# Attention with a 64-wide causal window and a ReGLU feed-forward: the first tile's matmuls in another order

## The chip, the cores and the metric

The kernel runs on one core of a Trainium2 chip. Its time is the device time of one execution in microseconds (us); three runs of the kernel before gave 301.91 (median), between 301.77 and 302.06. One further execution was recorded by the hardware profiler: all rows of the profile and of the trace are from it, and their times count from the start of its span.

The names in the profile: PE is TensorE's matmuls and PEld its weight loads, DVE is VectorE, ACT is ScalarE, POOL is GpSimd, SP is SyncE. L589 is line 589 of the kernel.

## What is computed

Two steps, one behind the other. First attention for 8 batches, 8 heads, 576 positions and 64 elements per head, in which a position sees itself and the 63 before it:

```python
scores = scale * np.matmul(q, k.transpose(0, 1, 3, 2))
mask = (rel >= 0) & (rel < 64)                  # rel = query position - key position
attn = softmax(np.where(mask, scores, -1e9))
attn_out = np.matmul(attn, v)
x = attn_out.transpose(0, 2, 1, 3).reshape(4608, 512)
```

then a gated feed-forward on its 4608 tokens of 512:

```python
gate = np.maximum(x @ w_gate, 0.0)              # w_gate 512 x 1536
val = x @ w_val                                 # w_val  512 x 1536
out = (gate * val) @ w_out                      # w_out 1536 x 512
```

Inputs and output are float32; the kernel's matmuls take fp16 and add up in fp32.

## The kernel before, in words

**Tiles and units.** The tokens are cut into small tiles of 384 at the start (`TT`) and large ones of 512 behind them (`WT`). A small tile has two units of 192 tokens (`U`); a unit is what attention works on: scores (`u_st`), exponentials on ScalarE (`u_exp`), masks on VectorE (`u_mask`), the product with v (`u_pv`), then the normalization by the sums (`u_recip`, `u_norm`) and a transposition (`u_turn`) that writes `xt`, the transposed input of the feed-forward. A unit's normalization and transposition come in two halves of four heads: the first half fills the chunks 0 and 1 of `xt`, the second half the chunks 2 and 3 (a matmul's contraction of 512 is done in 4 chunks of 128). For the second half of unit 1 the normalization is done on ScalarE by six operations (`u_norm_act`, L369), all else on VectorE.

**Feed-forward of the small tiles.** `hidden` (L557) computes outputs in blocks of 128 of the 1536, four at a time: first four of w_gate, each four matmuls (one per chunk, L589) into one of four PSUM banks that are taken in turn, with a ReLU by ScalarE to `pr` (L572) behind each; then the same four of w_val, with the product `pr` x bank by VectorE to `g_sb` behind each (the gate, L575). An output of w_gate in the next group writes a bank that a gate must have read before. For the first tile, `hidden(0, ((0, U), (U, TT)), 0, 4, 4)` does the first four outputs for unit 0 and then for unit 1, in matmuls of 192 tokens, two outputs to a bank; the other two groups of four take both units in matmuls of 384. Then come the first unit of the next tile, and `output`, the product with w_out (L1023). The large tiles use `fast_hidden`, `fast_output` and, for the last ones, the class around L847, which do the products by fewer, added-up submatrices named P1 to P7.

**Loads of weights.** `w_load` (L154) brings a group of four outputs in two transfers on GpSimd's queue: chunks 0 and 1, then chunks 2 and 3. All of these queue behind each other and behind loads of q, k and v on the same queue.

**Who sets the order.** Each engine runs its instructions in the order in which the program issues them. The class `Weaver` decides it when the program is built: it holds a clock and a heap of pieces of work with due times (`W.at`); `W.advance(t)` issues what is due until t and moves the clock on. `hidden` advances the clock by the length of its matmuls; `w_need` advances it to the time at which a weight group is planned to have landed (`w_done`). So a piece of attention, a transposition or a gate may be issued in another place when the clock changes upstream, although its own line does not. For the last large tiles the order of the pieces is written out by hand in `SEVEN` (L1069): P5a and P5b are two parts of P5, of four matmuls each, v0, v1, s0, s1 and h1 are pieces of attention and of the previous tile.

**What goes before.** The start (L1083 to L1135) computes the scores of units 0 and 1, with a few matmuls of no result (`heat`, `keep_hot`) between, normalizes and turns unit 0, then unit 1, issues the loads of the second and third groups of weights, and plans the scores of unit 2 at 23.2 on the planner's clock.

Of the kernel before, what the change touches and what calls it, by code (L numbers as in the profile page):

```python
# [10 lines left out]
FP32 = mybir.dt.float32  # L11
FP16 = mybir.dt.float16
ACT = mybir.ActivationFunctionType
MUL = mybir.AluOpType.mult
# [33 lines left out]
def kernel(  # L48
# [10 lines left out]
    nc = tc.nc  # L59
# [4 lines left out]
    U = 192  # L64
    UB = S // U
    NU = B * UB
    NC = DM // 128
    NF = DF // 128
    G = 4
    scale = 1.0 / float(D) ** 0.5  # L70
    TT = 2 * U
    WT = 512
# [12 lines left out]
    g_sb_p = ctx.enter_context(tc.tile_pool(name="g_sb", bufs=2))  # L85
    f_sb = ctx.enter_context(tc.tile_pool(name="f_sb", bufs=3))
# [6 lines left out]
    wg = persist.tile([128, NC, DF], FP16)  # L93
    wv = persist.tile([128, NC, DF], FP16)
# [46 lines left out]
    W = Weaver()  # L141
# [4 lines left out]
    def xt_tile(t):  # L146
        if t not in xts:
            xts[t] = x_sb.tile([128, NC, WT], FP16, name="xt")
        return xts[t]


    w_done = {}

    def w_load(wt, src, f0, f1, landed):  # L154

        if wt is not wo:
            ns = slice(128 * f0, 128 * f1)
            for a in range(2):
                nc.gpsimd.dma_start(wt[:, 2 * a:2 * a + 2, ns], src.rearrange("(a p e) n -> a p e n", a=2, e=2)[a, :, :, ns])  # L159
        if wt is wo:  # L160
            nc.gpsimd.dma_start(wo[:, f0:f1], src.rearrange("(c p) n -> p c n", p=128)[:, f0:f1])
        w_done.update(((wt.name, f), landed) for f in range(f0, f1))

    def w_need(wt, f):
        while (wt.name, f) not in w_done:
            W.pop()
        W.advance(w_done[wt.name, f])

# [52 lines left out]
    def heat(n, to, start=True):  # L223

        for _ in range(n):
            nc.tensor.matmul(to, zero[:, 0:128], zero[:, 0:to.shape[1]], start=start, stop=start, skip_group_check=not start)
# [9 lines left out]
    def one_bank():  # L236
        taken["one"] += 1
        to = singles[(taken["one"] - 1) % 4]
        while id(to) in unread:
            W.pop()  # L240
        return to
# [100 lines left out]
    def pv_of(d, u, hh):  # L342
        return d["pv"][hh][:, 0:SB * VW].rearrange("p (s c) -> p s c", c=VW)

    def u_recip(u, hhs=(0, 1)):
        d = units[u]
        if "r" not in d:
            d["r"] = a_n.tile([128, 2, SB, 1], FP32, name="r")
        for hh in hhs:
            nc.vector.reciprocal(d["r"][:, hh], pv_of(d, u, hh)[:, :, D:D + 1])  # L350

    def u_norm(u, hh):

        d = units[u]
        if "x" not in d:
            d["x"] = xus[:, u % 2].rearrange("p h (s e c) -> p h s e c", e=2, c=D // 2)
        nc.vector.tensor_tensor(d["x"][:, hh], pv_of(d, u, hh)[:, :, 0:D].rearrange("p s (c e) -> p s e c", e=2),
                                d["r"][:, hh, :, :, None].to_broadcast([128, SB, 2, D // 2]), MUL)
        if u >= 6:
            read(d["pv"][hh], True)  # L360

    def u_norm_act(u, hh):

        d = units[u]
        if "x" not in d:
            d["x"] = xus[:, u % 2].rearrange("p h (s e c) -> p h s e c", e=2, c=D // 2)
        pv = pv_of(d, u, hh)
        for s in range(SB):
            nc.scalar.activation(d["x"][:, hh, s], pv[:, s, 0:D].rearrange("p (c e) -> p e c", e=2), ACT.Copy,  # L369
                                 scale=d["r"][:, hh, s])  # L370

    def u_turn(u, hhs=(0, 1)):

        d = units[u]
        c0 = U * (u % 2)
        h0, h1 = hhs[0], hhs[-1] + 1
        for hh in range(h0, h1):
            dst = xt_tile(u // 2)[:, 2 * hh:2 * hh + 2, c0:c0 + U].rearrange("p e (s c) -> p s e c", c=32)
            nc.vector.transpose(dst, d["x"][:, hh])
        if h1 == 2:  # L380
            del units[u]
            if u < 4:
                normed[0] = (u + 1) // 2 - 1
            elif u % 2:
                for n in range(4):
                    W.at(W.clock + 0.5 + 0.9 * n, lambda n=n: x_form(u // 2, n))
# [20 lines left out]
    def part_written(banks):  # L407
        written.update((id(to), 0) for to in banks)

    def read(to, give):  # L410
        unread.discard(id(to))
        if give:
            free.append(to)
# [86 lines left out]
    def x_form(t, n):  # L500

        HT = widths[t] // 2
        xt, xc = xt_tile(t), xc_tile(t)[:, :, :, 0:HT]
        b11, b12, b21, b22 = (xt[:, 2 * k:2 * k + 2, HT * h:HT * h + HT] for k in range(2) for h in range(2))
        x, y = ((b12, b11), (b22, xc[:, 0]), (b22, b12), (b21, xc[:, 1]))[n]
        (nc.vector if t <= NS or t - 1 in FAST_OUT else nc.gpsimd).tensor_tensor(xc[:, n], x, y, SUB)
        if n == 3:
            normed[0] = t
# [42 lines left out]
    gs = {}  # L551
# [2 lines left out]
        while normed[0] < n:  # L554
            W.pop()

    def hidden(t, spans, f0=0, f1=NF, each=1):  # L557

        if t not in gs:
            gs[t] = g_sb_p.tile([128, NF, WT], FP16, name="g_sb"), {}  # L560
        g_sb, done = gs[t]
        xt = xt_tile(t)
        n = spans[0][1] - spans[0][0]

        w = 512 // n
        each = max(each, w)

        def part(tile):
            return tile[:, 0:w * n].rearrange("p (w n) -> p w n", w=w)

        def relu(r_sb, h1):
            nc.scalar.activation(part(r_sb), part(h1), ACT.Relu)  # L572

        def gate(f, c0, r_sb, h2):
            nc.vector.tensor_tensor(g_sb[:, f:f + w, c0:c0 + n], part(r_sb), part(h2), MUL)  # L575
            done.update(dict.fromkeys(range(f, f + w), c0 + n))

        for fb in range(f0, f1, each):
            r2s = [f_sb.tile([128, 2, WT], FP32, name="pr", bufs=4) for _ in range(2)]
            r_sbs = {}  # L580
            for i, wt in enumerate((wg, wv)):
                for c0, f in ((c0, f) for c0, _ in spans for f in range(fb, fb + each, w)):
                    h = one_bank()
                    part_written([h])
                    for b in range(w):
                        W.advance(W.clock)
                        w_need(wt, f + b)
                        for c in range(NC):
                            nc.tensor.matmul(h[:, b * n:b * n + n], wt[:, c, (f + b) * 128:(f + b) * 128 + 128],  # L589
                                             xt[:, c, c0:c0 + n], start=(c == 0), stop=(c == NC - 1))  # L590
                        W.clock += 4 * (n + 7) / 2400.0
                    if i == 0:
                        r_sb = r_sbs[c0, f] = r2s[len(r_sbs) // 2][:, len(r_sbs) % 2]
                        W.at(W.clock, lambda r_sb=r_sb, h=h: relu(r_sb, h))
                    else:
                        W.at(W.clock, lambda f=f, c0=c0, r_sb=r_sbs[c0, f], h=h: gate(f, c0, r_sb, h))

    def fast_hidden(t, seven=None):

# [418 lines left out]
    def out_mm(t, op, sub, f):  # L1018
        g_sb, done = gs[t]
        while done.get(f, 0) < sub * 128 + 128:  # L1020
            W.pop()
        w_need(wo, f)
        nc.tensor.matmul(op, g_sb[:, f, bass.ds(sub * 128, 128)], wo[:, f],  # L1023
                         start=(f == 0), stop=(f == NF - 1))
        W.clock += 519 / 2400.0
# [41 lines left out]
    XAT = -0.3  # L1067
    SEVEN_LAST = (("P6", "P5", "P2", "P7", "oP1", "P3", "P4"), ("P6", "P5", "P2", "P7", "oP1", "P4", "P3"))
    SEVEN = {n: ("P2", "v0", "v1", "P6", "P5a", "P7", "s0", "P5b", "P4", "s1", "P3") for n in (-5, -4, -3, -2)}  # L1069
    SEVEN[-1] = ("v0", "P2", "P6", "v1", "P5a", "P7", "P5b", "P4", "h1", "P3")  # L1070

    SEVEN[0] = ("P2", "P4", "P5", "P6", "P7", "P3")

    with tc.manual_schedule():
# [17 lines left out]
        v_load(0, ((1, 0, 128), (3, 0, 64)))  # L1092
        v_load(1, ((3, 64, 128), (5, 0, 128)))
        w_load(*G3[0], 15.2)
        w_load(*V3[0], 17.7)
        k_zeros()
        band_bias()
# [22 lines left out]
        for hh in range(2):  # L1120
            u_recip(0, (hh,))
            u_norm(0, hh)
        u_turn(0)
        for hh in range(2):
            u_pv(1, (hh,), True)
        heat(1, units[1]["st"][3])
        for hh in range(2):
            u_recip(1, (hh,))
        u_norm_act(1, 1)
        u_norm(1, 0)  # L1130
        for hh in range(2):
            u_turn(1, (hh,))
        w_load(*G3[1], 20.3)
        w_load(*V3[1], 22.8)
        v_load(2)  # L1135
# [113 lines left out]
                pass  # L1249

        W.advance(15.3)
        hidden(0, ((0, U), (U, TT)), 0, 4, 4)
        hidden(0, ((0, TT),), 4, NF, 4)
        hidden(1, ((0, U),), each=4)
        output(0, (0, 1), (0, 8, NF))
        ready(1)
# [78 lines left out]
```

## Time and profile before

| | us |
|---|---|
| median of three runs | 301.91 |
| the profiled execution's own time | 302.04 |
| its span (first to last instruction) | 300.3 |
| PE busy | 289.6 (96%) |
| DVE busy | 251.7 (84%) |
| POOL busy | 201.7 (67%) |
| ACT busy | 196.0 (65%) |

The profiled execution is 0.13 above the median, and 1.74 of its time lies outside the span. The row PEclk of the page gives the clock that TensorE was granted in each of 40 slices of the span, in tenths. A row of the timeline reads: start, time from the first start to the last end, engine, line, operation, output <- inputs, shapes, number of instructions, and in brackets the idle time ahead of it with what ended it. A matmul's end in these rows is modelled and its successor starts before it; so idle time of TensorE is counted here by starts: from one matmul's start to the next, less the usual distance of such matmuls. Where weights and inputs are there, 192-wide matmuls follow each other every 0.08 us and 384-wide ones every 0.16.

### The profile page before, as it was taken

The numbers are of one execution on the slowest core, as the hardware profiler recorded it, in microseconds if no ns is written. First come the engines' busy times: TensorE is split into PE (matmuls) and PEld (weight loads), VectorE is DVE, ScalarE is ACT, GpSimd is POOL, SyncE is SP. The second block draws the span as 40 slices with busy tenths as digits, with TensorE's granted clock in tenths as the row PEclk, the third lists the DMA queues.
The fourth block names the chain that finished last, engine by engine and source line by source line (L and its number), as shares of the span: only waits on it lengthen the run. The fifth ranks groups of instructions, "written<-read, shape, count | busy, mean of one in ns | idle before, by whom it ended". The sixth has DMA issues, their size and how long they took to land.

```text
span 300.3 us, 11073 instructions
## 1 busy us (share of the span) xinstructions
PE 289.6 (96%) x4643; PEld 239.4 (80%) x4643; DVE 251.7 (84%) x517; ACT 196.0 (65%) x408; POOL 201.7 (67%) x241
## 2 busy tenths in 40 slices
PE   4899999999999999999999999999999999999994
PEld 2475877748957975888888888888888888888894
DVE  5947895997995999789999899989858985896584
ACT  3545336258848848885798579857985698538850
POOL 8767689868957893985957595759375617441750
PEclk9999999999999999999999999999999999999999
DMA  7999999979919636911399239922911210031013
GB/s 216 183 196 194 194 197 179 160 131 241 80 40 181 164 70 149 146 42 38 61 219 120 60 53 219 126 57 53 173 37 35 74 41 0 3 103 41 0 38 105
DMA packets 59506, 33.20 MB, mean 111 GB/s; under 512 B 39552, under 2 KB 53824, under 8 KB 59456
## 3 DMA queue, kind: packets, MB, share of 16 engines
q0 software_dynamic: 46688, 18.29, 52.3%
q1 hardware_dynamic: 12192, 13.75, 15.1%
q8 instruction: 36, 0.59, 0.8%
q10 hardware_dynamic: 576, 0.46, 0.5%
q14 instruction: 14, 0.11, 0.1%
HBM read 37.75 MB, written 9.44 MB: 157 GB/s over the span
## 4 chain that ended last, share of the span: by engine, by line
PE 87%; DMA 5%; POOL 4%; DVE 2%; issue 1%; DVEq 0%; POOLq 0%
PE bank L634 46%; PE bank L847 17%; PE bank L589 7%; PE bank L767 5%; PE bank L1023 5%; PE bank L265 3%; DMA wg<-in_moe_w_gate_dram 3%; PE bank L465 2%; DMA v<-in_v_dram 2%; POOL v L205 1%; PE bank L336 1%; POOL wg L159 1%; DVE g_sb L659 1%; DVE g_sb L797 0%; POOL wv L159 0%
## 5 line engine op out<-in xcount | busy, mean ns | idle before, releaser
L659 POOL TENSOR_TENSOR g_sb<-pr 128x512 f16<-128x512 f32 (+1 forms) x36 | 42.7, 1193 | 43.6 <-ACT pr L676 43.6
L670 DVE TENSOR_TENSOR pr<-bank,pr 128x512 f32<-128x512 f32 (+1 forms) x96 | 58.5, 649 | 3.6 <-PE bank L634 1.9
L653 ACT COPY pr<-bank 128x512 f32<-128x512 f32 (+1 forms) x96 | 49.1, 566 | 13.7 <-PE bank L634 13.5
L659 DVE TENSOR_TENSOR g_sb<-r,bank 128x512 f16<-128x512 f32 (+1 forms) x48 | 31.3, 652 | 23.8 <-ACT r L703 22.4
L847 PEld LDWEIGHTS <-g_sb 128*128 128x128 f16 x444 | 41.8, 98 | 5.2 <-issue 0.2
L634 PE MATMUL bank<-xc,vs 128*128 128x256 f16 (+1 forms) x288 | 41.3, 266 | 0.0
L634 PE MATMUL bank<-xc,us 128*128 128x256 f16 (+1 forms) x288 | 41.3, 266 | 0.0
L634 PEld LDWEIGHTS <-vs 128*128 128x128 f16 x384 | 36.5, 98 | 3.5
L634 PEld LDWEIGHTS <-us 128*128 128x128 f16 x384 | 36.5, 98 | 3.3
L205 POOL DMA_DIRECT2D v<-in_v_dram x41 | 34.7, 866 | 2.2 <-DMA nats<-in_q_dram 1.0
L676 ACT ACTIVATE pr<-pr 128x512 f32<-128x512 f32 (+1 forms) x48 | 29.3, 610 | 9.8 <-DVE pr L670 9.8
L703 ACT ACTIVATE r<-bank 128x512 f32<-128x512 f32 (+1 forms) x48 | 27.7, 577 | 4.8 <-PE bank L634 4.0
L634 PEld LDWEIGHTS <-wg 128*128 128x128 f16 x288 | 27.4, 98 | 3.2
L634 PEld LDWEIGHTS <-wv 128*128 128x128 f16 x288 | 27.4, 98 | 2.6
L634 PE MATMUL bank<-xt,wg 128*128 128x256 f16 (+1 forms) x192 | 27.5, 266 | 0.0
L634 PE MATMUL bank<-xt,wv 128*128 128x256 f16 (+1 forms) x192 | 27.5, 266 | 0.0
L797 POOL TENSOR_TENSOR g_sb<-g_sb,xus 128x512 f16<-128x512 f16 x24 | 27.1, 1148 | 0.0
L847 PE MATMUL bank<-wo,g_sb 128*128 128x256 f16 (+1 forms) x222 | 26.6, 270 | 0.0
L430 ACT ACTIVATE pw<-bank 128x512 f16<-128x512 f32 x48 | 25.3, 605 | 1.1 <-PE bank L265 0.7
L847 PE MATMUL bank<-wts,g_sb 128*128 128x256 f16 (+1 forms) x222 | 25.4, 270 | 0.2 <-DVE xw L484 0.2
L643 ACT COPY bank<-bank 128x512 f32<-128x512 f32 (+1 forms) x48 | 24.6, 553 | 0.0
L572 ACT ACTIVATE pr<-bank 128x384 f32<-128x384 f32 x24 | 11.9, 501 | 15.5 <-PE bank L589 12.5
(107 smaller groups left out, 559.8 us busy)
## 6 DMA issues: line engine op xcount, KB each, us to landing
out_dram<-o_sb SPq DMA_DIRECT2D x30, 256.0 KB, 3.1
nats<-in_k_dram POOLq DMA_DIRECT2D x15, 288.0 KB, 6.1
nats<-in_q_dram POOLq DMA_DIRECT2D x15, 288.0 KB, 8.0
v<-in_v_dram POOLq DMA_DIRECT2D x31, 128.0 KB, 8.2
v<-v SPq DMA_DIRECT2D x27, 66.0 KB, 2.7
v<-v SPq DMA_DIRECT2D x13, 132.0 KB, 2.5
wg<-in_moe_w_gate_dram POOLq DMA_DIRECT2D x6, 256.0 KB, 6.4
wv<-in_moe_w_val_dram POOLq DMA_DIRECT2D x6, 256.0 KB, 8.1
```

Of the source, the lines that this page charges most:

```text
L205: nc.gpsimd.dma_start(v16s[b % 2][lo:hi, g, :, 0:64], v[b, :, 64 * g - 64 + lo:64 * g - 64 + hi].rearrange("h p d -> p h d"))
L430: nc.scalar.activation(d["p"][g].rearrange("p n c -> p (n c)"), d["st"][g], ACT.Exp, scale=scale)
L589: nc.tensor.matmul(h[:, b * n:b * n + n], wt[:, c, (f + b) * 128:(f + b) * 128 + 128], xt[:, c, c0:c0 + n], start=(c == 0), stop=(c == NC ...
L634: nc.tensor.matmul(to[:, HT * m:HT * m + HT], w[:, k, 128 * m:128 * m + 128], x[:, k], start=(first and m == 0 and k == 0), stop=(k == 1), ...
L643: nc.scalar.copy(at[j, "B", i][:, 0:TW], at[j, "A", i][:, 0:TW])
L653: nc.scalar.copy(pr[:, i], at[j, "A", i][:, 0:TW])
L659: eng.tensor_tensor(gh[:, f:f + 2, h], pair(r), pair(v), MUL)
L670: nc.vector.tensor_tensor(pr[:, i], to[:, 0:TW], pr[:, i], ADD)
L676: nc.scalar.activation(pr[:, 0], pr[:, 0], ACT.Relu)
L703: nc.scalar.activation(r, to[:, 0:TW], ACT.Relu)
L797: eng.tensor_tensor(to, x, y, op)
L847: nc.tensor.matmul(at[key][:, QN * m * whole:QN * m * whole + n1 - n0], A[:, 128 * m:128 * m + 128], B[:, c, n0:n1], start=(first and m == ...
```

## The change

Five edits.

1. `w_done` and `w_need` know the two halves of a weight group apart; the first is planned 1.3 us ahead of the second.
2. The first four outputs of the first tile are issued by a new function `first_hidden`. For w_gate: outputs 0 and 1 for unit 0; outputs 2 and 3, each for both units in matmuls of 384, both over the chunks 0 and 1 and then both over 2 and 3; outputs 0 and 1 for unit 1. For w_val the same four blocks one after the other, in matmuls of 192.
3. `hidden` gets `halves`: the first so many outputs of a group are done over the chunks 0 and 1 for all of them, then over 2 and 3. It is used for two outputs of w_val in the second group, for all four of w_gate and two of w_val in the third. And `split`: the w_gate outputs 4 and 5 are done in two matmuls of 192 per chunk.
4. The second unit's normalization: the reciprocal of its second half comes first, ahead of the transposition of unit 0's second half; then the reciprocal of its first half.
5. The last tile's list has P5 whole and behind P7.

```diff
-        w_done.update(((wt.name, f), landed) for f in range(f0, f1))
+        w_done.update(((wt.name, f, a), landed - 1.3 * (1 - a)) for f in range(f0, f1) for a in range(2))
...
-    def hidden(t, spans, f0=0, f1=NF, each=1):
+    def hidden(t, spans, f0=0, f1=NF, each=1, halves={}, split=()):
...
+                items = [(c0, f) for c0, _ in spans for f in range(fb, fb + each, w)]
+                first = halves.get((fb, i), 1)
+                for group in [items[:first]] + [[item] for item in items[first:]]:
+                    hs = [one_bank() for _ in group]
+                    part_written(hs)
+                    for cs in ((0, 1), (2, 3)) if len(group) > 1 else (range(NC),):
+                        for (c0, f), h in zip(group, hs):
+                            for b in range(w):
+                                W.advance(W.clock)
+                                w_need(wt, f + b, cs[-1] // 2)
+                                m = n // 2 if i == 0 and f in split else n
...
+    def first_hidden():
...
+        blocks = (((0, 0), (1, 0)), ((2, 0), (2, 1)), ((3, 0), (3, 1)), ((0, 1), (1, 1)))
...
+        for i, then in enumerate((relu, gate)):
+            for group in ((0,), (1, 2), (3,)) if i == 0 else ((0,), (1,), (2,), (3,)):
+                hs = [one_bank() for _ in group]
+                part_written(hs)
+                for cs in ((0, 1), (2, 3)):
+                    for n, h in zip(group, hs):
+                        products(h, i, blocks[n], cs)
+                        if cs[-1] == NC - 1:
+                            W.at(W.clock, lambda n=n, h=h, then=then: then(n, h))
...
-    SEVEN[-1] = ("v0", "P2", "P6", "v1", "P5a", "P7", "P5b", "P4", "h1", "P3")
+    SEVEN[-1] = ("v0", "P2", "P6", "v1", "P7", "P5", "P4", "h1", "P3")
...
-        u_turn(0)
+        u_turn(0, (0,))
         for hh in range(2):
             u_pv(1, (hh,), True)
         heat(1, units[1]["st"][3])
-        for hh in range(2):
-            u_recip(1, (hh,))
+        u_recip(1, (1,))
         u_norm_act(1, 1)
+        u_turn(0, (1,))
+        u_recip(1, (0,))
         u_norm(1, 0)
...
-        hidden(0, ((0, U), (U, TT)), 0, 4, 4)
-        hidden(0, ((0, TT),), 4, NF, 4)
+        first_hidden()
+        hidden(0, ((0, TT),), 4, NF, 4, split=(4,5,), halves={(4, 1): 2, (8, 0): 4, (8, 1): 2})
```

Each engine's number of instructions of work stays as it is on TensorE (the 384-wide matmuls of the first group and the split of outputs 4 and 5 balance); GpSimd's order does not change. On TensorE, VectorE, ScalarE and SyncE the planner issues several pieces between about 20 and 70 us in another order.

More of the change, by code (lines that the diff above doesn't have):

```diff
@@ L161, in w_load, with w_need @@
             nc.gpsimd.dma_start(wo[:, f0:f1], src.rearrange("(c p) n -> p c n", p=128)[:, f0:f1])
-        w_done.update(((wt.name, f), landed) for f in range(f0, f1))
-    def w_need(wt, f):
-        while (wt.name, f) not in w_done:
+        w_done.update(((wt.name, f, a), landed - 1.3 * (1 - a)) for f in range(f0, f1) for a in range(2))
+    def w_need(wt, f, a=1):
+        while (wt.name, f, a) not in w_done:
             W.pop()
-        W.advance(w_done[wt.name, f])
+        W.advance(w_done[wt.name, f, a])
     nat = {}
@@ L581, in hidden @@
             for i, wt in enumerate((wg, wv)):
[L582 to L596, printed above, removed]
+                items = [(c0, f) for c0, _ in spans for f in range(fb, fb + each, w)]
@@ new lines, in hidden @@
+                first = halves.get((fb, i), 1)
[8 more added lines that the diff above has]
+                                m = n // 2 if i == 0 and f in split else n
+                                for c, lo in ((c, lo) for c in cs for lo in range(0, n, m)):
+                                    nc.tensor.matmul(h[:, b * n + lo:b * n + lo + m], wt[:, c, (f + b) * 128:(f + b) * 128 + 128],
+                                                     xt[:, c, c0 + lo:c0 + lo + m], start=(c == 0 and lo == 0 and not (len(group) > 1 and b)),
+                                                     stop=(c == NC - 1), skip_group_check=len(group) > 1 or m < n)
+                                W.clock += len(cs) * (n + 7) / 2400.0
+                            if cs[-1] < NC - 1:
+                                continue
+                            if i == 0:
+                                r_sb = r_sbs[c0, f] = r2s[len(r_sbs) // 2][:, len(r_sbs) % 2]
+                                W.at(W.clock, lambda r_sb=r_sb, h=h: relu(r_sb, h))
+                            else:
+                                W.at(W.clock, lambda f=f, c0=c0, r_sb=r_sbs[c0, f], h=h: gate(f, c0, r_sb, h))
@@ new lines, in first_hidden, with products, relu, gate @@
+    def first_hidden():
+        g_sb, done = gs[0] = g_sb_p.tile([128, NF, WT], FP16, name="g_sb"), {}
+        xt = xt_tile(0)
+        r2s = [f_sb.tile([128, 2, WT], FP32, name="pr", bufs=4) for _ in range(2)]
+        r_sbs = [r2s[n // 2][:, n % 2, 0:TT] for n in range(4)]
+        blocks = (((0, 0), (1, 0)), ((2, 0), (2, 1)), ((3, 0), (3, 1)), ((0, 1), (1, 1)))
+        parts = lambda tile: tile.rearrange("p (w n) -> p w n", w=2)
+        def products(h, i, block, cs):
+            wt = (wg, wv)[i]
+            W.advance(W.clock)
+            w_need(wt, block[-1][0], cs[-1] // 2)
+            whole = i == 0 and block[0][0] == block[1][0]
+            for c in cs if whole else ():
+                nc.tensor.matmul(h[:, 0:TT], wt[:, c, block[0][0] * 128:block[0][0] * 128 + 128], xt[:, c, 0:TT],
+                                 start=(c == 0), stop=(c == NC - 1), skip_group_check=True)
+            for n, (f, u) in () if whole else enumerate(block):
+                for c in cs:
+                    nc.tensor.matmul(h[:, U * n:U * n + U], wt[:, c, f * 128:f * 128 + 128], xt[:, c, U * u:U * u + U],
+                                     start=(c == 0 and n == 0), stop=(c == NC - 1), skip_group_check=True)
+            W.clock += 2 * len(cs) * (U + 7) / 2400.0
+        def relu(n, h):
+            nc.scalar.activation(r_sbs[n], h[:, 0:TT], ACT.Relu)
+        def gate(n, h):
+            (f, u), (f1, u1) = blocks[n]
+            if f == f1:
+                to = g_sb[:, f:f + 1, 0:TT]
+                nc.vector.tensor_tensor(to, r_sbs[n].rearrange("p (w n) -> p w n", w=1), h[:, 0:TT].rearrange("p (w n) -> p w n", w=1), MUL)
+                done[f] = TT
+            else:
+                nc.vector.tensor_tensor(g_sb[:, f:f + 2, U * u:U * u + U], parts(r_sbs[n]), parts(h[:, 0:TT]), MUL)
+                done.update({f: U * u + U, f1: U * u + U})
+        for i, then in enumerate((relu, gate)):
[7 more added lines that the diff above has]
+                            W.at(W.clock, lambda n=n, h=h, then=then: then(n, h))
```

## The prediction

> **What bounds the kernel now.** I read the page first (busy shares, slices, chain), then the list of TensorE's waits between 12 and 70 us, then the timeline of the two stretches where those waits lie, then the order in which the two programs issue each engine's instructions.
>
> ```profile
> PE 289.6 (96%) x4643; PEld 239.4 (80%) x4643; DVE 251.7 (84%) x517; ACT 196.0 (65%) x408; POOL 201.7 (67%) x241
> PEclk9999999999999999999999999999999999999999
> PE 87%; DMA 5%; POOL 4%; DVE 2%; issue 1%; DVEq 0%; POOLq 0%
> ```
>
> TensorE is busy for 96% of the span, at the full granted clock, and the chain that ends last is TensorE for 87%. Nothing but TensorE's idle time is there to be won. Between 12 and 70 us the waits list has two lines:
>
> ```profile
> PE bank L589 <- DMA wg<-in_moe_w_gate_dram: 0.7, 2, 0.4
> PE bank L589 <- DVE xt L379: 0.7, 1, 0.7
> ```
>
> The first lists two waits, for the second half of a w_gate group; the second is one wait for the turned second unit. The timeline of the first one and of the turned unit:
>
> ```profile
> 14.51 1.33 PE L589 MATMUL bank<-xt,wg 128*128 128x192 f16 x14 [0.35 <-DMA wg<-in_moe_w_gate_dram]
> 14.95 0.58 DVE L379 STREAM_TRANSPOSE xt<-xus 128x384 f16<-128x384 f16 x1
> 15.80 0.58 DVE L379 STREAM_TRANSPOSE xt<-xus 128x384 f16<-128x384 f16 x1 [0.27 <-ACT xus L369]
> 16.50 1.48 PE L589 MATMUL bank<-xt,wg 128*128 128x192 f16 x16 [0.66 <-DVE xt L379]
> 17.82 2.80 PE L589 MATMUL bank<-xt,wv 128*128 128x192 f16 x32
> ```
>
> The pitch of a 192-wide matmul is (20.45-17.82)/32 = 0.082 us (the w_gate row after it starts at 20.45), so by starts TensorE loses 16.50-14.51-14x0.082 = 0.84 us before 16.50. The third group of w_gate:
>
> ```profile
> 23.63 2.77 PE L589 MATMUL bank<-xt,wv 128*128 128x384 f16 x16
> 23.75 1.64 ACT L299 ACTIVATE p<-bank 128x384 f16<-128x384 f32 x4
> 24.10 1.70 POOL L215 COPY v<-v 64x512 f16<-64x512 f16 x2 [3.05 <-DMA v<-in_v_dram]
> 24.56 0.56 DVE L575 TENSOR_TENSOR g_sb<-pr,bank 128x384 f16<-128x384 f32 x1 [3.28 <-PE bank L589]
> 25.03 1.25 DVE L306 TENSOR_TENSOR p<-p,mask 128x384 f16<-128x384 f16 x2
> 26.24 0.49 PE L589 MATMUL bank<-xt,wg 128*128 128x384 f16 x2
> 26.67 0.61 DVE L306 TENSOR_TENSOR p<-p,mask 128x384 f16<-128x384 f16 x2
> 27.09 0.50 PE L589 MATMUL bank<-xt,wg 128*128 128x384 f16 x2 [0.36 <-DMA wg<-in_moe_w_gate_dram]
> 27.20 1.00 DVE L575 TENSOR_TENSOR g_sb<-pr,bank 128x384 f16<-128x384 f32 x2
> 27.52 0.56 PE L336 MATMUL bank<-v,p 128*32 128x65 f16 x48
> 28.01 2.12 PE L589 MATMUL bank<-xt,wg 128*128 128x384 f16 x12
> 29.97 2.76 PE L589 MATMUL bank<-xt,wv 128*128 128x384 f16 x16
> ```
>
> The pitch of a 384-wide matmul is (29.97-28.01)/12 = 0.163 us, so the hole before 27.09 is 27.09-26.24-2x0.163 = 0.52 us. What the reader is to see beside it: VectorE works without a break from 24.56 to 28.20, through four gates and four masks, and the last two gates free the banks that the third and fourth output of this w_gate group write. Before, those two banks are written only behind the attention of unit 2 (27.52), at about 28.7 and 29.3, long after.
>
> **First group.** Removed: the sixteen matmuls of unit 0 and then sixteen of unit 1. Put in their place: 8 of 192 (two outputs, unit 0), 8 of 384 (two outputs, both units, first over chunks 0 and 1, then 2 and 3), 8 of 192 (unit 1). The columns are the same. On VectorE the reciprocal of unit 1's second half now stands ahead of the second transposition of unit 0 and of the other reciprocal. It waits for that half's attention, which ends at about 13.80, so it runs at 13.88 rather than 14.3; ScalarE's six operations (14.43, 1.34 us) move to about 14.06 to 15.40. The transposition of unit 0's second half moves from 13.71 to 13.96 and ends at 14.49; the matmuls behind it wait for weights until 14.47 anyway, so that costs 0.03. Then reciprocal (to 14.61), normalization 0.56 and transposition 0.58 of the first half: 14.95 becomes 15.20, done 15.78; the second half is turned at 15.69 to 16.22 (before: to 16.38). TensorE: 8 narrow matmuls end at 14.54+4x0.082 = 14.87, it idles to 15.83, then 4x0.163 = 16.48, by when the second half is turned, 4x0.163 = 17.14, 8x0.082 = 17.80. w_val therefore starts at 17.80 and not 17.82: 0.02 gained. Idle time is moved, not removed.
>
> **Third w_gate group.** Its four outputs are now all computed over chunks 0 and 1, then the attention of unit 2, then all over chunks 2 and 3. That hides the landing at 27.05: 8x0.163 = 1.31 us of work from 26.22 would reach 27.53, and -0.52 would follow. But the third and fourth bank are now wanted at 26.87 and 27.20, and VectorE frees them at 27.7 and 28.2 in the rows above. In the changed order VectorE has the same eight operations, but the first mask comes first, and may start when the first exponential is done, at 23.75+0.49 = 24.24, in place of the gate at 24.56. The same 3.65 us of work then ends at 24.26+3.65 = 27.91. TensorE writes the fourth bank from 27.95, and everything behind stands in its queue: 2 matmuls 0.33, change to attention and attention and back 27.52-27.42+28.01-27.52 = 0.59, 8 matmuls 1.31. w_val starts at 27.95+2.23 = 30.18, against 29.97: a loss of 0.21 where the diff removes a wait of 0.52. Who waits: unit 2's reciprocals (28.13 becomes about 28.8), its transpositions (to about 31.0); they are wanted by the next tile at 32.57, so this is covered.
>
> Bounds: the price that I do not see is that of the masks. Two at 25.03 took 1.25, two at 26.67 took 0.61; the first pair ran beside GpSimd's copies (24.10, 1.70 for two). If the moved mask takes 0.3 like the later pair, the last gate ends at about 27.63 (it can't before 27.1, since its own w_val output ends at about 26.5), and w_val starts at 29.91: -0.06. If both early masks are slowed like the worst (0.98 of the 1.25), it ends at about 28.43, and w_val starts at 30.71: +0.74. I take +0.21, the row's own total, since mask and copies overlap in both orders. The Trainium skill ("SBUF — State Buffer", section Who interferes with whom) says that a VectorE operation with both inputs in SBUF contends with a GpSimd operation that reads SBUF, and that the later one is blocked for the whole instruction. The slow pair agrees; but the copies, 0.60 and then 1.04 us, were stretched too. By full blocking until the second copy ends at 25.80, the last gate would end at about 28.7, the loss here be 1.0 and the time 302.8.
>
> **w_val by halves, split outputs 4 and 5.** w_val of groups two and three starts at 23.6 and 30.2, after both its halves are there (no wait in the list): 0. The split is 16 matmuls of 192 for 8 of 384, 16x0.082 against 8x0.163: 0.01.
>
> **What the planner moves behind that (31 to 70 us).** Scores of unit 3 come 8 narrow matmuls (0.66) later, those of units 4 and 5 likewise, those of 6 and 7 three output matmuls (0.65) later; gates pass ahead of the transpositions of k and q. TensorE has two stalls of 0.03 and 0.06 there (33.92, 37.00), which go; as much can come back at the q transposition, due at 37.4 on both sides: -0.05. A gate of 0.47 now stands ahead of unit 5's last mask, which was done only just in time; its reader is 0.66 later: bound 0 to 0.4, taken +0.05. w_out lands at 42.0 and 44.56, 1.0 us ahead of its use; nothing there. GpSimd's order is unchanged. SyncE issues one store ahead of four spreads of v, which are 0.6 later and wanted some 3 us on: 0.
>
> **Last tile.** P5a's four matmuls go behind P7.
>
> ```profile
> 263.59 0.81 PE L847 MATMUL bank<-wts,g_sb 128*128 128x256 f16 x6 [0.18 <-DVE xw L484]
> ```
>
> This row's matmuls wait for xw; P7's bank is free when ScalarE's copy ends at 263.41. Between 0 and -0.18; taken -0.09.
>
> **Sum.** -0.02+0.21-0.05+0.05-0.09 = +0.10. The profiled execution took 302.04 (span 300.3 and 1.74 around it), 0.13 above the median; so 302.14 in a profile, 302.0 as a median. 0.2% (0.6 us) is about what the measurement of this kernel can tell from no change.
>
> **Rivals.**
> 1. The third group's wait vanishes as the diff reads: sum -0.02-0.52-0.05+0.05-0.09 = -0.63, 301.3. It needs the last gate done by 27.2, when its own input is ready only at 26.5 and VectorE has four masks to do between. Chance 0.11; another 0.02 for more than that.
> 2. Slower: VectorE's masks both meet the copies: +0.74 in place of +0.21, 302.5. It decides when the last gate ends after 28.3. Chance 0.15.
> 3. Slower: in the first group TensorE starts again only when both halves of unit 1 are turned. For this speaks the row at 16.50: its first matmul needs only the half that was turned at 15.53, and yet all sixteen start at once, 0.12 after the other half. Against it: the weight load ahead of it, which waits for nothing, was also held to 16.50, so that something else stopped TensorE's queue. Start 16.34, w_val at 16.34+1.31+0.66 = 18.31, +0.5; masks and gates then follow from 24.75, and the third group ends as late again: +0.6 to +0.7, 302.6. Chance 0.13.
> 4. The clock drops in the first group's idle time (0.37+0.96 us): its 1.97 us of work would take twice that (the 384-wide matmuls at 4.68 to 6.60 us started 0.32 apart): 304. Before idles 0.3+0.84 there with full PEclk. Chance 0.03. The Trainium skill ("TensorE: Matmul & The Clock Gate", Part 1) puts the half clock behind an idle window of about 3.4 us, which speaks against it.
>
> **Numbers.** Forecast, within 0.2%: 0.56. Faster 0.13 (rival 1). Slower 0.31 (rivals 2 to 4). The range goes from 301.4 (the mask bound -0.06 with the tail's -0.18 gives 301.6; half of rival 1 beside it) to 302.7 (rivals 2 and 3).
>
> **What would show it.** Right: no wait on w_gate's DMA at 27, but two on VectorE's gates, 0.6 to 0.8 together, and the third w_val from about 30.2; w_val of the first group from 17.8; the 384-wide pair from 15.8. Wrong: the last gate of the second group done by 27.3 (faster), or after 28.4 (slower), or the first group starting again at 16.3.

## The result, and the profile after

The changed kernel takes 302.47 us (median of 14 executions, 301.94 to 302.82) where the kernel before takes 301.87 (14 executions, 301.66 to 302.45): a ratio of 1.0017, 95% interval 1.0009 to 1.0025. A second measurement of the same two, on the chip of the second set of experiments, gives 302.27 against 301.91: 1.0011, interval 1.0003 to 1.0020. By the medians the change costs 0.4 to 0.6 us. That is within 0.2%, as forecast, and inside the range, but with little to spare: both intervals lie above 1, so it is a loss, and the predicted 302.0 is 0.3 to 0.5 too low.

One thing has to be said before the profile is read: the profiled execution took 301.94 us, less than the 302.04 of the profiled execution of before. It is the fastest of the 14; eight others took 302.42 to 302.82, and executions of 302.4 and more are the "slow runs" of the expectations below. What follows reads this trace first and then says what it doesn't show.

The page of the changed kernel: busy shares, granted clock, chain.

```profile
PE 290.4 (97%) x4643; PEld 239.7 (80%) x4643; DVE 251.3 (84%) x517; ACT 196.3 (65%) x408; POOL 201.3 (67%) x241
PEclk9999999999999999999999999999999999999999
PE 94%; DVE 3%; POOL 1%; issue 1%; ACT 0%; DVEq 0%; POOLq 0%
```

The clock never dropped. The transfers, 5% of the chain before, are no longer in it, and VectorE has 3%. TensorE's waits between 12 and 70 us:

```profile
PE bank L625 <- DMA wg<-in_moe_w_gate_dram: 0.6, 1, 0.6
PE bank L621 <- DVE xt L379: 0.4, 1, 0.4
PE bank L594 <- DVE g_sb L575: 0.2, 1, 0.2
```

The two waits for w_gate's transfers have become one, and a wait for VectorE's gates is new. The timeline of the first group (L621 and L625 are `first_hidden`'s matmuls):

```profile
13.81 0.49 PE L625 MATMUL bank<-xt,wg 128*128 128x192 f16 x4
14.90 0.50 PE L625 MATMUL bank<-xt,wg 128*128 128x192 f16 x4 [0.60 <-DMA wg<-in_moe_w_gate_dram]
15.19 1.04 DVE L379 STREAM_TRANSPOSE xt<-xus 128x384 f16<-128x384 f16 x2
15.82 1.46 PE L621 MATMUL bank<-xt,wg 128*128 128x384 f16 x8 [0.42 <-DVE xt L379]
17.78 2.80 PE L625 MATMUL bank<-xt,wv 128*128 128x192 f16 x32
```

The 384-wide matmuls start at 15.82 (predicted 15.83), when only the first half of unit 1 is turned, and w_val starts at 17.78 (predicted 17.80). w_gate's second half landed 0.4 later in this execution than in the one before, which costs nothing here: the wait for the turned unit behind it is the later one. The third group of w_gate:

```profile
23.84 0.60 POOL L215 COPY v<-v 64x512 f16<-64x512 f16 x1 [2.71 <-DMA v<-in_v_dram]
24.26 0.39 DVE L306 TENSOR_TENSOR p<-p,mask 128x384 f16<-128x384 f16 x1 [3.02 <-ACT p L299]
24.50 1.06 POOL L215 COPY v<-v 64x1024 f16<-64x1024 f16 x1
25.28 0.49 DVE L306 TENSOR_TENSOR p<-p,mask 128x384 f16<-128x384 f16 x1
26.23 0.81 PE L594 MATMUL bank<-xt,wg 128*128 128x384 f16 x4
26.69 1.00 DVE L575 TENSOR_TENSOR g_sb<-pr,bank 128x384 f16<-128x384 f32 x2
27.29 0.95 PE L594 MATMUL bank<-xt,wg 128*128 128x384 f16 x4 [0.24 <-DVE g_sb L575]
28.17 0.56 PE L336 MATMUL bank<-v,p 128*32 128x65 f16 x48
28.66 1.47 PE L594 MATMUL bank<-xt,wg 128*128 128x384 f16 x8
29.97 2.76 PE L594 MATMUL bank<-xt,wv 128*128 128x384 f16 x16
```

Here is the wait that took the other's place. TensorE does two half-outputs from 26.23, stands still until the third bank is free (27.29: 27.29-26.23-4x0.163 = 0.41), and loses another 0.14 at 27.75 on the fourth; the attention of unit 2 waits behind it in the queue. The third w_val starts at 29.97, to the hundredth where it started before; that the two times are equal is chance, as the other traces will show.

### The profile page after: what moved, and what is told of

Read it like the earlier page. It is cut to its first block, busy times and chain, and to the rows that moved or that the text cites. A ratio compares the mean times of both kernels' runs of the same rounds, so it can differ in the third digit from the quotient of the medians.

```text
span 300.2 us, 11073 instructions
## 1 busy us (share of the span) xinstructions
PE 290.4 (97%) x4643; PEld 239.7 (80%) x4643; DVE 251.3 (84%) x517; ACT 196.3 (65%) x408; POOL 201.3 (67%) x241
## 4 chain that ended last, share of the span: by engine, by line
PE 94%; DVE 3%; POOL 1%; issue 1%; ACT 0%; DVEq 0%; POOLq 0%
PE bank L688 46%; PE bank L901 18%; PE bank L594 8%; PE bank L821 5%; PE bank L1077 5%; PE bank L265 4%; PE bank L465 2%; PE bank L336 1%; PE bank L625 1%; PE bank L232 1%; PE bank L229 1%; DVE xt L379 1%; DVE xus L357 1%; DVE g_sb L575 0%; PE bank L621 0%
## 5 line engine op out<-in xcount | busy, mean ns | idle before, releaser
L199 DVE STREAM_TRANSPOSE qT<-nats 128x576 f32<-128x576 f32 x16 | 19.7, 1241 | 0.1
```

## The experiments

The theories on record are: T1, VectorE's gates are late in the third w_gate group and the half-outputs stand in TensorE's queue; T2, the loss is in the first group; T3, behind 31 us; later T4 (VectorE's chain to unit 5's masks) and T5 (a store holds a buffer).

**1. The third w_gate group as before.**

```diff
- halves={(4, 1): 2, (8, 0): 4, (8, 1): 2}
+ halves={(4, 1): 2, (8, 1): 2}
```

> The changed kernel with the third w_gate group output by output again, as before (no halves there; all other edits stay). The profiled execution of the changed kernel took 301.94 us, yet 8 of its 14 runs took 302.4 to 302.8. Theory T1: in those runs VectorE's masks are slowed beside GpSimd's copies and the gates free the third and fourth bank late, while the four half-outputs stand in TensorE's queue. Then this kernel has no such runs: 301.9, within 0.15 of before, with the wait of 0.4 to 0.5 us on w_gate's transfer back at about 27 us. Rival T2: the runs are slow in the first group (a later landing or a later start on the second unit): about 302.4 here too. Rival T3: they are slow behind 31 us, where the planner has moved scores, masks and gates: about 302.4 here too.

Measured 301.86 (11 executions, none above 302.10) against 301.95 of before: 0.9994, interval 0.9985 to 1.0003. The whole loss is gone, as T1 said. The wait on the transfer did not come back, though:

```profile
24.38 1.19 DVE L306 TENSOR_TENSOR p<-p,mask 128x384 f16<-128x384 f16 x1 [3.02 <-ACT p L299]
26.35 0.81 PE L594 MATMUL bank<-xt,wg 128*128 128x384 f16 x4
27.09 0.80 PE L336 MATMUL bank<-v,p 128*32 128x65 f16 x48
27.82 2.12 PE L594 MATMUL bank<-xt,wg 128*128 128x384 f16 x12
29.78 0.98 PE L594 MATMUL bank<-xt,wv 128*128 128x384 f16 x5
```

The four matmuls of the first output run through from 26.35 with no wait between chunks 1 and 2: the second half landed at 26.60 in this execution, against 27.05 in the profiled one of before. In the two further traces of kernels with the old order up to here (experiments 4 and 10) it landed at 26.71 and 26.73, and there is no wait there either. The wait that the edit removes is thus there in one of the five traces of kernels that do this group output by output (experiment 11 is the fifth); the one on the gates, in all six traces of kernels that have the edit and keep unit 2's masks up to here (0.41 to 0.67 on the third bank and 0.14 on the fourth). The attention of unit 2 takes 0.80 here and 0.56 elsewhere: it waits for a mask, since the first mask met GpSimd's copies and took 1.19.

**2. Two outputs by halves, not four.**

```diff
- (8, 0): 4
+ (8, 0): 2
```

> The changed kernel with two outputs of the third w_gate group by halves, not four: the third and fourth bank are then wanted only behind the attention of unit 2, as before. T1: neither wait is left in full: the half landing at about 27.05 comes 0.1 to 0.2 us behind the four half-matmuls that hide it or behind unit 2's attention, so w_val starts at about 29.5 and not 29.97: 0.3 to 0.45 faster than before, 301.5. T2 and T3: 0.4 of that is gained in the fast runs, the slow ones keep their 0.5: about 302.0.

Measured 302.00; 1.0000, 0.9990 to 1.0009. The mechanism came as T1 has it, the time did not:

```profile
29.54 2.76 PE L594 MATMUL bank<-xt,wv 128*128 128x384 f16 x16
55.08 1.28 PE L336 MATMUL bank<-v,p 128*32 128x65 f16 x96
55.82 0.42 PEld L336 LDWEIGHTS <-p 128*32 128x32 f16 x45 [0.20 <-DVE p L306]
```

w_val starts at 29.54, 0.43 ahead of the changed kernel. At 55.08 the attention of units 4 and 5 takes 1.28, where it took 1.06 before (at 54.56) and 1.20 in the changed kernel: it waits for unit 5's last mask on VectorE. Part of what TensorE gains at 30 us it gives back at 56.

**3. The first group and the normalization as before.** The call of `first_hidden` and the split go, the old `hidden(0, ((0, U), (U, TT)), 0, 4, 4)` and the old order of reciprocals come back.

> The changed kernel with the first group and the second unit's normalization as before (and without the split of outputs 4 and 5, so that TensorE's instruction count stays); halves, the two halves' due times and the last tile's list stay changed. T1: slow runs as in the changed kernel, about 302.3 to 302.5. T2: no slow runs, 301.9 to 302.0. T3: as T1.

Measured 302.07; 1.0003, 0.9993 to 1.0012: between what T1 and T2 said, and not to be told from either kernel. The trace has the gate wait (27.57, 0.41 and 0.14) and the old stop in the first group (16.76), and its third w_val starts at 30.25.

**4. The last tile's list alone.**

```diff
- SEVEN[-1] = ("v0", "P2", "P6", "v1", "P5a", "P7", "P5b", "P4", "h1", "P3")
+ SEVEN[-1] = ("v0", "P2", "P6", "v1", "P7", "P5", "P4", "h1", "P3")
```

> The kernel before with the last tile's list alone changed (P5 whole and behind P7). All theories: TensorE's stall at about 263.6 us goes from 0.35 to 0.2 us, so 0.1 faster than before (between 0 and 0.18): 301.8.

Measured 301.85 against 301.95; 0.9996, 0.9987 to 1.0005. The sign and size are as expected, the interval doesn't separate them. In the changed kernel the stop there is 0.22 by starts instead of 0.35.

**5. The changed kernel once more.**

> The changed kernel itself, to see on one chip with the next three which of its runs are slow and, if the profiled one is, where. Theory T1 (gates behind slowed masks in the third w_gate group): a slow run has TensorE restarting after 28.3 us there. Theory T4 (new, from the first four traces): VectorE's first masks of unit 4 at about 48.9 us end 0.2 us behind GpSimd's operation of L528 in all six traces (49.74 to 50.13), VectorE then works without a break, and unit 5's last mask releases TensorE's attention at about 55.8: a slow run has that mask later, after 56. Median 302.2 to 302.5 by either.

Measured 302.27 (see above). The profiled execution took 302.56, one of the three of 302.4 and more among eleven, and its third group is that of the first trace (27.35, w_val from 30.03). Neither theory explains it: TensorE goes on at 27.35 and not after 28.3 (T1), and unit 5's last mask is done at 55.96, 0.15 later than in the first trace, with 1.28 for the attention instead of 1.20 (T4): 0.08 of the 0.62 between the two executions. What it has beside that is at 77 us. ScalarE and TensorE there, and the last store of the small tiles:

```profile
77.17 0.86 ACT L707 COPY pr<-bank 128x384 f32<-128x384 f32 x2 [0.35 <-PE bank L688]
77.70 0.49 PE L688 MATMUL bank<-xc,wg 128*128 128x192 f16 x4 [0.26 <-ACT pr L707]
out_dram<-pr SPq DMA_DIRECT2D x1, 256.0 KB, 6.9
```

In the first trace of the changed kernel the same two are

```profile
76.55 0.87 ACT L707 COPY pr<-bank 128x384 f32<-128x384 f32 x2
out_dram<-pr SPq DMA_DIRECT2D x1, 256.0 KB, 5.1
```

ScalarE's copy writes the buffer that this store reads. Issued at 70.16 and 6.9 us on its way, it lands at 77.09, and the copy starts at 77.17; TensorE stops for 0.43 at 77.70. (The releaser in brackets is not the one that counts: this trace is 0.15 behind the first at 70.16, so that by its matmuls the copy would start at 76.70.) That the store holds the copy is read from these two times in one trace. T5 was made from this.

**6. Without unit 2's masks.** `plan_exps(23.2, 2, mask=False)`.

> The changed kernel without the four masks of unit 2 (left out, so that unit 2's attention takes unmasked weights). T1: the wait on VectorE's gates at 27.3 us (0.4+0.14) goes or falls under 0.1, the third w_val starts at 29.5, and no run is slow: 301.6 to 301.9. T4: w_val starts at 29.5 as well, but the 0.45 is not kept: VectorE's chain from 48 us still ends at 55.8, and TensorE waits there 0.3 to 0.5 instead of 0.14: 302.1 to 302.4, slow runs stay.

Measured 301.93; 1.0002, 0.9992 to 1.0013 (the ratio leaves out an execution of 1357.25). That is nearer to T1 in the median, though 302.43 and 303.15 are among its executions.

```profile
24.88 2.18 DVE L575 TENSOR_TENSOR g_sb<-pr,bank 128x384 f16<-128x384 f32 x4 [3.63 <-PE bank L594]
26.23 1.46 PE L594 MATMUL bank<-xt,wg 128*128 128x384 f16 x8
29.43 2.76 PE L594 MATMUL bank<-xt,wv 128*128 128x384 f16 x16
```

With VectorE free for the gates, the eight half-matmuls run without a stop, and w_val starts at 29.43, which is 26.22+1.31+0.59+1.31, the sum that the diff promises. The halves work if the banks are free. Of the 0.54 about 0.3 is left at the start of the fourth tile (68.86 instead of 69.20).

**7. Without unit 5's masks.** `plan_exps(T, u, mask=(u != 5))`.

> The changed kernel without the four masks of unit 5 (left out). T1: the waits at 27.3 us stay and so do the slow runs; 0.05 faster than the changed kernel. T4: no wait in unit 5's attention and VectorE 1.2 us ahead behind it: 0.15 to 0.5 faster than the changed kernel, no slow runs, about 301.8 to 301.9.

Measured 302.10; 1.0009, 1.0001 to 1.0018. 0.17 below the changed kernel of the same set, at the edge of what T4 said, and with four of twelve executions over 302.4 all the same. The attention of units 4 and 5 takes 1.06 there, without a wait, so unit 5's masks are not what makes them.

**8. Without GpSimd's small copies behind unit 3's masks.** The line `W.at(40.6, lambda: behind_masks(3))` goes.

> The changed kernel without GpSimd's four small copies that wait for unit 3's masks (behind_masks(3), about 41.2 to 42.9 us), so that its seven L528 operations run 1.3 to 2 us earlier and end at about 48.3, before unit 4's masks. T4: unit 4's first mask takes 0.4 and not 1.2, VectorE's chain ends 0.5 or more earlier, the wait in unit 5's attention goes; in exchange unit 3's masks at 40 to 42 meet L528: between 0.3 faster and 0.2 slower than the changed kernel. T1: nothing changes at 27 us; same time as the changed kernel within 0.1.

Measured 305.55 (6 executions): 1.0113, 1.0094 to 1.0133. No theory had 3.3 us. VectorE's masks of unit 3, one of GpSimd's operations beside them and TensorE's attention behind them:

```profile
40.60 2.21 DVE L306 TENSOR_TENSOR p<-p,mask 128x192 f16<-128x192 f16 x4
43.20 1.86 DVE L306 TENSOR_TENSOR p<-p,mask 128x192 f16<-128x192 f16 x2
43.78 1.16 POOL L528 TENSOR_TENSOR us<-wg 128x512 f16<-128x512 f16 x1
45.12 0.35 PE L336 MATMUL bank<-v,p 128*32 128x65 f16 x21 [0.92 <-DVE p L306]
```

The same masks in the changed kernel:

```profile
40.09 1.25 DVE L306 TENSOR_TENSOR p<-p,mask 128x192 f16<-128x192 f16 x4
41.72 0.42 DVE L306 TENSOR_TENSOR p<-p,mask 128x192 f16<-128x192 f16 x2
```

With GpSimd's L528 operations beside them the last two masks take 1.86 and not 0.42. TensorE waits 1.5 us for masks here, in two places, and at 58.65 and 59.32 another 0.8 for transfers of v; why those come late was not followed.

**9 to 12. The last small store from another buffer**, alone and with the edits of experiments 1 and 2:

```diff
-            if t == 0:
+            if t == 0 or sub == 2:
                 o_sb = f_sb.tile([128, DM], FP32, name="o_sb")
```

On the changed kernel:

> The changed kernel, with the last store of the small tiles taken from an o_sb buffer and not from a pr buffer, so that ScalarE's copy at about 76.5 us has no store to wait for. Theory T5 (from the slow trace of the changed kernel): the slow runs are those in which that store, issued at about 70.1, lands after 76.5 (77.09 in that trace, 75.15 in the fast one) and holds ScalarE's copy and TensorE 0.4 us. Then no run here is over 302.3 and the median is 302.0 to 302.1, 0.2 to 0.4 below the changed kernel. Rival T4 (the slow runs come from VectorE's chain and unit 5's masks): median 302.3 to 302.5 and slow runs as before.

Measured 302.45 against 301.94; 1.0017, 1.0007 to 1.0027. Seven of its twelve executions take 302.4 and more, so T5 falls as the cause of these. There is no stop at 77 us in the trace, but this profiled execution took 302.93, because it started late:

```profile
11.27 1.49 DVE L215 COPY v<-v 64x512 f16<-64x512 f16 x4 [0.62 <-DMA v<-in_v_dram]
14.69 1.09 PE L625 MATMUL bank<-xt,wg 128*128 128x192 f16 x8
30.80 1.46 PE L594 MATMUL bank<-xt,wv 128*128 128x384 f16 x8
```

v of unit 0 landed late: VectorE's first copy of it waited for a transfer until 11.27, where it started at 10.48 in the first trace of the changed kernel, and the first tile's first matmul came at 14.69 instead of 13.81, and the third w_val at 30.80 instead of 29.97: 16.11 and 16.16 behind it. On the kernel before:

> The kernel before with the same other buffer for the last store. T5: its store lands at 75.7 where it is wanted at 76.4, so only its rare slow runs (302.3 and more, 4 to 8 in 30) go: median 301.8 to 301.9, at most 0.1 faster. T4: no difference.

Measured 302.10; 1.0004, 0.9995 to 1.0013: no gain, against T5. With experiment 1:

> The changed kernel without halves in the third w_gate group, with the other buffer for the last store. T5: 301.75 to 301.85, 0.1 to 0.2 faster than before. T4: as without the buffer, 301.86.

Measured 301.85 against 301.94; 1.0011, 0.9990 to 1.0031 (one execution of 305.58 widens it), and T4 and T5 are not told apart. This run and experiment 9 differ in nothing but the halves of the third w_gate group and were measured on one chip: 301.85 without them, 302.45 with them. With experiment 2:

> The changed kernel with two outputs of the third w_gate group by halves, with the other buffer for the last store. T5: 301.85 to 301.95, without the runs of 302.6 to 302.8 that it had. T4: 302.0, those runs stay. By both, TensorE is 0.4 us ahead of the kernel before at 30 us and has lost it to unit 5's masks by 57 us.

Measured 301.71 against 301.94; 0.9999, 0.9990 to 1.0007. By its median the fastest, but no version here is shown to beat the kernel before.

**All traces on one measure.** The start of an execution moves by up to 0.9 us, so the distance from the first tile's first matmul to the third w_val tells more than either time. Each column is one way to do the third w_gate group (experiment 6, without unit 2's masks, is not in it):

| | output by output | two by halves | four by halves |
|---|---|---|---|
| old first group | 16.13 (before), 16.02 (exp. 4), 15.76 (exp. 10) | | 16.39 (exp. 3) |
| new first group | 15.81 (exp. 1), 15.63 (exp. 11) | 15.57 (exp. 2), 15.53 (exp. 12) | 16.16, 16.16 (changed), 16.29 (exp. 7), 16.16 (exp. 8), 16.11 (exp. 9) |

Down a column the new first group saves about 0.2. Along the lower row four outputs by halves cost 0.3 to 0.65 against none, and two save about 0.15. The trace of before, against which the prediction was made, is the slowest of its cell.

Farther on the picture is simpler. The fourth tile starts with these matmuls, in the kernel before and in the changed one:

```profile
69.08 0.49 PE L634 MATMUL bank<-xt,wg 128*128 128x192 f16 x4
69.20 0.49 PE L688 MATMUL bank<-xt,wg 128*128 128x192 f16 x4
```

The distance from the first tile's first matmul to this one (without experiment 8, which loses its time in between):

| | output by output | two by halves | four by halves |
|---|---|---|---|
| old first group | 55.24 (before), 55.13 (exp. 4), 54.88 (exp. 10) | | 55.46 (exp. 3) |
| new first group | 55.10 (exp. 1), 54.90 (exp. 11) | 55.19 (exp. 2), 54.86 (exp. 12) | 55.39, 55.48 (changed), 55.57 (exp. 7), 55.48 (exp. 9) |

The gain of the new first group and that of two outputs by halves are gone by then, as far as the spread within a cell lets one tell; the loss of four outputs by halves is still 0.3 to 0.65. Of the first group's gain about 0.17 goes shortly before 33.9 us in experiments 1 and 11: sixteen matmuls of 192 take 1.54 and 1.53 us there up to the next start, against 1.36 and 1.37 in experiments 4 and 10. That fits the medians of experiments 1 and 4, 301.86 and 301.85.

## Why the prediction was right, and where it was off

- **First group, step right, term too small.** The starts came to within 0.02 us. Rival 3 (a start only when both halves are turned) did not happen, as the reason given against it says: the stop at 16.50 was not for VectorE, as far as the rows show (below). But -0.02 was taken against one trace; the old order goes on at 16.50 to 17.03 in four traces, and the first table gives the new one about -0.2. By the second table nothing of it is left at the fourth tile where the third group is done output by output.
- **Third w_gate group, mechanism right, both its prices off.** The forecast was that a wait for the gates takes the place of the wait for the transfer, 0.6 to 0.8 together, with w_val at 30.18. Measured 0.55 and 29.97: the moved mask met only the short copy and took 0.39, the next one the end of the long copy (0.49). What failed is the other side of the balance, "the hole before 27.09 is 0.52 us", taken as what every execution loses. The transfer landed at 27.05 in that one, and at 26.60 to 26.73 in four other traces of kernels without the four halves (experiments 1, 4, 10 and 11), which have no hole; 27.05 is the latest of all traces. So in place of +0.21 stand +0.3 to +0.65. Experiment 1, which undoes only this, takes the loss back, and experiment 11 does so against experiment 9 on one chip: that it carries the loss is shown.
- **31 to 70 us.** Place right: the attention of unit 5 waits for its last mask, 1.20 against 1.06 us, +0.14 for the +0.05 taken. From the third w_val to the fourth tile the old order takes 39.11 or 39.12 in three traces, the changed kernel 39.23 and 39.32. The trace shows VectorE without a break behind unit 4's first mask:

```profile
48.75 1.16 POOL L528 TENSOR_TENSOR vs<-wv,vs 128x512 f16<-128x512 f16 x1
48.88 1.24 DVE L306 TENSOR_TENSOR p<-p,mask 128x384 f16<-128x384 f16 x1 [3.81 <-ACT p L299]
55.20 1.20 PE L336 MATMUL bank<-v,p 128*32 128x65 f16 x96
55.48 0.33 DVE L306 TENSOR_TENSOR p<-p,mask 128x384 f16<-128x384 f16 x1
```

- **Last tile.** -0.09 taken, 0.35-0.22 = 0.13 found.
- **The sum.** -0.2, then +0.3 to +0.65, +0.14, -0.13: +0.1 to +0.5 for +0.10, where the medians have +0.4 to +0.6. That the forecast of a time within 0.2% held owes something to luck: terms that were too small on both sides cancel in part. The stop at 77 us (0.43, in one of two traces of the changed kernel) was in no step; that it happens is shown, how often is not.
- **Rival 1** (faster, 0.13) failed on the gates, as argued; experiment 6 shows that it is right but for them. **Rival 2** (both early masks slowed) did not come. In experiment 7 one of them took 1.04, the other 0.35, and w_val came 16.29 behind the first matmul: 0.13 more than in the first trace, not 0.5. Its 28.43 is also not what its words give: 0.98 for the other mask of 0.27 adds 0.71, and 27.91 becomes 28.62. **Rival 4:** full clock throughout.

Open: why eight of fourteen executions lie at 302.4 and above. With experiments 5 and 9 it is 18 of 37, and 8 of 111 of the kernel before, so it goes with the change; by experiments 1 and 11 (none and one, of 23) it goes with the four halves, though it is only 2 of 11 in experiment 3, which has them beside the old first group. Two traces of the changed kernel and experiments 7 and 9 give three single causes (a store landing late, v landing late, a slowed mask). The first matmul comes late (14.40 to 14.69) in experiments 7, 8 and 9, three of the seven traces with four halves, and in none of the other seven (13.84 to 13.97); nothing seen here explains why. The traces with four halves pass it on, since their waits are on other engines and move with it, while the transfer doesn't move as far (26.90 in experiment 9, which starts 0.88 later, against 26.63); that fits, but no late start of the kernel before was profiled.

## What to carry to other kernels

A transfer waited for in one trace may have landed in the next: before hiding it, see the wait in several executions. Work put ahead of a wait needs its output buffers earlier, so ask who empties them and when. And compare traces by distances between landmarks, not by clock times, where the start varies by more than the effect.

## What the runs showed of the hardware

**TensorE stood still once, at a nearly fixed distance behind a transfer of instructions.** In the four traces with the old first group a transfer on queue 8 (instruction, 16 KB each on the page) begins at 14.15, 14.45, 14.64 and 14.44 us, and unit 1's first matmul starts at 16.50, 16.76, 17.03 and 16.76: 2.35, 2.31, 2.39 and 2.32 behind. Its operands were ready 1.0 to 1.4 us earlier. In experiment 4:

```profile
15.91 0.58 DVE L379 STREAM_TRANSPOSE xt<-xus 128x384 f16<-128x384 f16 x1 [0.27 <-ACT xus L369]
17.03 1.48 PE L589 MATMUL bank<-xt,wg 128*128 128x192 f16 x16 [1.20 <-DVE xt L379]
17.03 1.25 PEld L589 LDWEIGHTS <-wg 128*128 128x128 f16 x15 [1.34 <-issue]
```

The half that it needs is turned by 15.64, the other by 16.49; the weight load ahead of it waits for nothing ("issue") and is held as well. In the new order the matmul at that place of the program is due only at 17.1, and there is no stop. That this transfer brings TensorE's instructions and that it is the cause is argued from these distances; no run changed the fetch alone. The Trainium skill ("Runtime: NRT & Kernel Launch", Instruction fetch mechanics) says that instructions come in blocks of 16 KiB over a queue of the sequencer's own, mostly hidden; here, if the argument holds, one block was not.

**VectorE's masks end 0.1 to 0.2 us behind GpSimd's operation that they met.** The mask in the third group ended at 24.65, the copy beside it at 24.44; the next mask at 25.77, the long copy at 25.56; in experiments 7 and 9 the masks of 1.04 and 0.85 us ended 0.2 behind a copy; the mask at 48.88 ended at 50.12, the L528 operation beside it at 49.91. The masks of 128x192 in experiment 8 end 0.11 behind (45.06 and 44.95). The Trainium skill ("SBUF — State Buffer", Who interferes with whom) says that such a mask contends with a GpSimd operation that reads SBUF, and that what the two share is an exclusive lock; these rows agree. The prediction doubted it because the copies took 0.60 and 1.04: they are of different sizes (64x512 and 64x1024 in the rows above), which the grouped row hid. It also let the mask wait for both copies; it waited for the one that was running. How much it can cost, experiment 8 shows: TensorE waits 1.5 us for masks in a kernel that takes 3.3 us more (305.55 against 302.27).
